# Fused attention, mixture of experts and MLP: another order for the first and last attention slots, and weight loads held back behind the second expert's tokens

## The chip, the cores and the metric

The kernel runs on 1 core of one Trainium2 chip. The metric is device time of the whole program in microseconds (us). TensorE is PE, VectorE DVE, ScalarE ACT, GpSimd POOL and SyncE SP. SP computes nothing; it issues most of the DMAs, in the order of the program. Each engine works off its own queue strictly in order. Where a queue is meant that only issues DMAs, the profile writes SPq, ACTq or POOLq.

## The reference, cut to what matters

Three stages follow each other: a decayed linear attention in blocks, a mixture of 8 experts of which each token takes one, and an MLP.

```python
for b in range(nb):                                  # attention, 2 batches x 8 heads, 768 x 64
    intra = (qb @ kb.T * Dmask) @ vb
    inter = (qb * lam_pow) @ kv_state
    out[:, :, sl] = intra + inter
    kv_state = lam_block * kv_state + (kb * rev_pow).T @ vb
x = out as [1536 tokens, 512]
logits = (x / |x|) @ (emb / |emb|).T / tau           # routing: 8 experts, the largest wins
for e in range(8):
    out[mask_e] = gate_w * (relu(x[mask_e] @ w1[e]) @ w2[e])      # 512 -> 1024 -> 512
h = x @ w_in; g = elu(h); y = g @ w_out              # 512 -> 2048 -> 512
```

## The kernel before, in words

**Attention in slots.** The 1,536 tokens are 12 slots of 128 (6 chunks of 128 positions, 2 batches; slot s is chunk s // 2 of batch s % 2). A slot's q, k and v arrive as one 1 MB tile in two DMAs of 512 KB (`load_a`, `load_b`, L333 to L344). Per slot there are these steps, each a nested function of `attention`:

- `stage_a` (L346, PE): keys times queries into the PSUM tile `st`. `mask` (L357, DVE): two multiplications of `st` with the decay mask `Dm` into `stm`. `keys` and `queries` (L365, L374, POOL): decayed keys `kd` and queries `qd`.
- `stage_b` (L382, PE): state `St` times `qd` (L390) and values times `stm` (L397) into `xp`; ACT then copies it to `xs` (L402). The state has to be up to date for the slot two before.
- `products` (L409, PE L417, POOL L422) and `add` (L426, DVE L432): the slot's contribution to the state.
- `stage_c` (L434), a generator that is advanced one step at a time. Step 1: PE turns `xs` into token-major form and takes the expert logits with it, into `tm` (L439, "the turn" below). Step 2: DVE sums the logits `lg` (L443). Step 3: ACT squares, accumulates and takes the root (L448, L449). Steps 4 and 5: DVE `nrm` and `rs` (L451, L455). Step 6: ACT writes the normalised row's upper half (L459). Step 7: DVE the lower half (L462), and SP writes the row to the DRAM tensor `rows` (L465), twice for slots 0 to 3.

The order is written out by hand: the program order is the order of each engine's queue. In the loop over s (L507 to L538) slot s does `queries`, `stage_a`, `mask`, `keys`, then `stage_c(s - 2)`, `stage_b(s - 1)` and `products(s - 1)`. Slots 10 and 11 and the routing are a list written out after the loop (L540 to L575).

**Start.** `powers` (L273) makes the decay powers `zs` and writes them from ACT's queue to a DRAM tensor `Z`; `masks` (L288) reads `Z` back as a skewed view, from SP's queue, into `Dm`. SP has issued slots 0 and 1 before that and issues slots 2 to 5 behind it.

**Weights.** Every weight piece (1 MB of float32) is loaded into one of 5 raw buffers by `load` (L125) and split by `preparing` (L147) into two float16 halves, in two chunks a piece: an ACT operation (L157, 128x1024) for the upper half and, one step later, a DVE operation (L161) for the lower. A chunk that ends a piece calls `load` for the next one. In attention, `ATT_LOADS` and `ATT_STEPS` (L50, L51) name the slots in which a load or one step is put between the attention work; later `tick` (L206) hands out steps by a budget.

**Routing and the first expert.** `top` and `route` (L607, L631) find each token's expert and its place among that expert's tokens, by small DVE operations and small PE products, here for the slot groups 0 to 7, 8 to 10 (`top` in two parts) and 11. `first_gather` (L674) makes indices of expert 0's tokens in slots 0 to 7 and fetches them from `rows` by two indirect DMAs of POOL (`gather`, L765; 128 rows, then 96 rows of 2 KB). `dispatch` (L699) adds those of slots 8 to 11 by one-hot products on PE (L721) and gives expert 0's tokens `x`.

**Experts.** `layer1(e)` (L937) has 96 matrix products for each expert (L949), `layer2(e)` 96 (L990), in the order layer1(0), layer1(1), layer2(0), layer1(2), ... After the first 24 of layer1(0), `route_end` (L753) makes the indices of all the other experts and issues `gather(1)`; after 72, `transpose(1)` turns the gathered tokens of expert 1 on PE (L933) and ACT copies them (L934). Later experts' tokens are turned by a DMA.

`manual_schedule` keeps this order, and two engines that touch one PSUM tile are kept in program order by semaphores, two readers too, as the trace shows for the tile `tm`.

Of the kernel before, what the change touches and what calls it, by code (L numbers as in the profile page):

```python
# [21 lines left out]
P = 128  # L22
# [27 lines left out]
ATT_LOADS = (2, 4, 5, 6, 7)  # L50
ATT_STEPS = range(4, 8)  # L51
# [14 lines left out]
class K:  # L66
    def __init__(self, ctx, tc, A, out, dbg=None):
        self.ctx, self.tc, self.nc, self.A, self.out = ctx, tc, tc.nc, A, out
        self.dbg = dbg or {}
        self.raws = {}  # L70
        self.wts = {}
        self.next_load = 0
        self.rings = [], []
        self.hold = False
# [50 lines left out]
    def load(self):  # L125

        if self.next_load >= len(self.units):
# [19 lines left out]
    def preparing(self):  # L147
# [21 lines left out]
        for i, h in self.units:  # L169
            while h == 0 and (self.hold or not self.w_free()):  # L170
# [5 lines left out]
            while (i, h) not in self.raws:  # L176
                self.load()
# [128 lines left out]
    def attention(self, ctx):  # L306
# [26 lines left out]
        def load_a(s):  # L333
# [6 lines left out]
            nc.sync.dma_start(t[:, 0:2], A["qkv"][s, :, 0:2])  # L340
            T[s] = t

        def load_b(s):
            return nc.sync.dma_start(T[s][:, 2:4], A["qkv"][s, :, 2:4])  # L344
# [60 lines left out]
        def state(s):  # L405
            products(s)
            add(s)

# [25 lines left out]
        def stage_c(s):  # L434
            xs = XS.pop(s)

            tm = ps_s.tile([P, KD, 256], F32, name=f"tm{s}", tag="st")
            for k in range(KD):
                nc.tensor.matmul(tm[:, k, 0 : P + E], xs[:, k, :], ie[:, k, :], start=True, stop=True)  # L439
            yield  # L440
            x = tm[:, :, 0:P]
            g = slice(s, s + 1)
            nc.vector.tensor_reduce(  # L443
                out=lg[:, s, :], in_=tm[:, :, P : P + E].rearrange("p k e -> p e k"), axis=AX.X, op=ALU.add
            )
            yield
            sq = ap.tile([P, KD, P], F32, name=f"sq{s}", tag="sq", bufs=1)
            nc.scalar.activation(out=sq, in_=x, func=AF.Square, accum_out=ss[:, g])  # L448
            nc.scalar.activation(out=yr[:, g], in_=ss[:, g], func=AF.Sqrt)  # L449
            yield  # L450
# [3 lines left out]
            yield  # L454
            nc.vector.reciprocal(out=rs[:, g], in_=nrm[:, g])  # L455
            yield
            row = ap.tile([P, 2, DM], F16, name=f"row{s}", tag="row", bufs=NS - FIRST)
            hi, lo = (row[:, j].rearrange("p (k c) -> p k c", c=P) for j in range(2))
            nc.scalar.activation(out=hi, in_=x, func=AF.Copy, scale=rs[:, g])  # L459
            self.row[s] = row  # L460
            yield
            nc.vector.scalar_tensor_tensor(out=lo, in0=x, scalar=rs[:, g], in1=hi, op0=ALU.mult, op1=ALU.subtract)  # L462
# [13 lines left out]
        for s in range(2):  # L476
            load_a(s)
            load_b(s)
        warm(6)
        zt, zs = self.powers(a1, ps_r)  # L480
        self.masks(a1, zt)
        self.scales(a1, zs)
        load_a(2)
        load_b(2)
        nc.scalar.dma_start(self.c32[:, 128:], A["c32"][:, 128:])
        for s in range(3, 6):
            load_a(s)
            load_b(s)
# [17 lines left out]
        run = lambda g: [None for _ in g]  # L506
        for s in range(1, 10):  # L507
            if s > 1:
                if s in IN_AT:
                    load_a(IN_AT[s])  # L510
                    load_b(IN_AT[s])
                if s in ATT_LOADS:
                    self.load()
                queries(s)
                if s > 2:
                    stage_a(s)
                mask(s)
                keys(s)
            c = stage_c(s - 2) if s > 1 else iter(())
            if s == 2:  # L520
                next(c), next(c)
                stage_b(s - 1)
                run(c)
            else:
                if s > 3:


                    next(c), next(c), next(c)
                    add(s - 2)
                    next(c), next(c)  # L530
                    if s in ATT_STEPS:
                        self.step()
                run(c)
                stage_b(s - 1)
            state(s) if s == 1 else s > 2 and products(s - 1)
# [4 lines left out]
        c8, c9, c10, c11 = (stage_c(s) for s in range(8, NS))  # L540
        t7, t9, t10, t11 = (self.top(*g, a1) for g in ((0, 8), (8, 10), (10, 11), (11, 12)))
        r7, r10, r11 = (self.route(*g, a1, ps_r) for g in ((0, 8), (8, 11), (11, 12)))
# [3 lines left out]
        go(t7, t7, t7, t7)  # L546
        queries(10)
        stage_a(10)
        mask(10)
        go(r7, c8, c8)  # L550
        add(8)
        go(c8, r7, r7, r7, c8, c8)
        stage_b(9)
        products(9)
        go(fg, c8, fg, c8)
        queries(11)
        stage_a(11)
        mask(11)
        self.group += 1
        go(c9, c9)  # L560
        add(9)
        go(c9, fg, fg, c9, c9)
        stage_b(10)
        self.finished("in10")
        go(t9, t9, t9, t9, c9, c9)
        self.step()
        go(c10, c10, t10, c10, t10, c10, t10, c10, t10)
# [3 lines left out]
        go(r10, r10, put, c10, c10)  # L571
        self.step()

# [762 lines left out]
```

## Time and profile before

| | us |
|---|---|
| median of 3 runs (504.83 to 507.26) | 506.09 |
| the profiled execution's own time | 507.02 |
| its span | 505.1 |
| PE busy (share of the span) | 471.9 (93%) |
| DVE busy | 345.1 (68%) |
| ACT busy | 230.1 (46%) |
| POOL busy | 73.0 (14%) |

Times below are from the start of the span. In a line of the timeline the columns are the start, the duration, engine, line, operation, the tiles written and read, the count, and in brackets how long the engine had been idle and what ended that.

### The profile page before, as it was taken

To read this page: it belongs to the slowest core of one execution; us is meant where nothing else is said; L and a number is where in the kernel's file an instruction comes from. 1 tells how busy PE (TensorE), PEld (TensorE's weight loads), DVE (VectorE), ACT (ScalarE), POOL (GpSimd) and SP (SyncE) were. 2 spreads that over 40 slices of the span, in tenths; PEclk is the share of its full clock that TensorE was granted. 3 is DMA by queue.
4 is the path that set the end of the run, shared out by engine and by line. 5 is a ranking of instruction groups with operands and counts; after the bars stand their busy time and mean duration, and the time that the engine had idled before them with its cause. 6 is when DMAs were issued, how large, how long until landed. Compare 5 with 4: busy or idle time off the path is not lost. (4 is left out here: it accounts for less than half of the span.)

```text
span 505.1 us, 9103 instructions
## 1 busy us (share of the span) xinstructions
PE 471.9 (93%) x3678; PEld 332.3 (66%) x3678; DVE 345.1 (68%) x612; ACT 230.1 (46%) x382; POOL 73.0 (14%) x66
## 2 busy tenths in 40 slices
PE   6789976689999999999999999999999999999993
PEld 6688865589999999999644444444444444445561
DVE  3469775849999957999787897889544435345352
ACT  1156433768785665333364444535242333333341
POOL 4359520502103100000000000000000003003020
PEclk9799987979999999999999999999999999999997
DMA  6999923599999979956522220000000002002010
GB/s 220 377 404 405 404 96 126 202 283 307 303 381 295 345 289 307 328 182 215 190 84 83 84 84 1 0 1 1 0 1 0 1 0 84 0 2 84 1 62 27
DMA packets 27959, 79.09 MB, mean 157 GB/s; under 512 B 13280, under 2 KB 14848, under 8 KB 21768
## 3 DMA queue, kind: packets, MB, share of 16 engines
q1 hardware_dynamic: 25280, 70.63, 41.2%
q0 software_dynamic: 2288, 7.61, 4.2%
q8 instruction: 31, 0.51, 0.4%
q10 hardware_dynamic: 344, 0.21, 0.2%
q14 instruction: 16, 0.13, 0.1%
HBM read 68.33 MB, written 7.36 MB: 150 GB/s over the span
## 5 line engine op out<-in xcount | busy, mean ns | idle before, releaser
L1034 PE MATMUL pf<-yT,w 128*128 128x512 f16 (+2 forms) x672 | 133.4, 349 | 0.6 <-DVE yT L1000 0.6
L1074 PE MATMUL po<-w,g 128*128 128x512 f16 x576 | 133.3, 379 | 0.3 <-DVE g L1060 0.3
L1034 PEld LDWEIGHTS <-w 128*128 128x128 f16 x672 | 62.4, 98 | 66.0 <-issue 0.9
L1044 DVE TENSOR_TENSOR et<-pf,bc 128x512 f32<-128x512 f32 (+2 forms) x56 | 34.4, 615 | 97.0 <-PE pf L1034 94.8
L1074 PEld LDWEIGHTS <-g 128*128 128x128 f16 x576 | 55.9, 98 | 66.1 <-DVE g L1060 1.2
L1045 ACT ACTIVATE eu<-et 128x512 f32<-128x512 f32 (+2 forms) x56 | 31.9, 569 | 139.8 <-DVE et L1044 139.8
L161 DVE SCALAR_TENSOR_TENSOR w<-raw,w 128x1024 f16<-128x1024 f32 x64 | 76.6, 1228 | 17.8 <-ACT w L157 17.8
L949 PE MATMUL ph<-x,w 128*128 128x224 f16 x768 | 76.9, 262 | 0.5 <-DVE x L749 0.5
L949 PEld LDWEIGHTS <-w 128*128 128x128 f16 x768 | 74.6, 99 | 1.5 <-issue 0.7
L990 PE MATMUL py<-h,w 128*128 128x224 f16 x768 | 74.7, 259 | 0.0
L990 PEld LDWEIGHTS <-w 128*128 128x128 f16 x768 | 73.4, 98 | 0.2 <-issue 0.2
L157 ACT ACTIVATE w<-raw 128x1024 f16<-128x1024 f32 x64 | 64.4, 1051 | 2.2 <-DVE cs L882 2.1
L1093 POOL DMA_INDIRECT out<-o,idx x12 | 12.0, 1004 | 285.4 <-DVE o L1091 276.8
L769 POOL DMA_INDIRECT g<-rows,idx x16 | 22.8, 1428 | 91.0 <-DMA x<-g 60.0
L1060 DVE SCALAR_TENSOR_TENSOR g<-et,g 128x512 f16<-128x512 f32 (+2 forms) x56 | 34.0, 608 | 0.2 <-ACT g L1054 0.2
L1053 DVE SCALAR_TENSOR_TENSOR et<-eu,et 128x512 f32<-128x512 f32 (+2 forms) x56 | 33.9, 605 | 0.3 <-ACT eu L1046 0.3
L1046 ACT ACTIVATE eu<-eu 128x512 f32<-128x512 f32 (+2 forms) x56 | 31.9, 570 | 1.8
L1054 ACT ACTIVATE g<-et 128x512 f16<-128x512 f32 (+2 forms) x56 | 30.9, 552 | 0.2 <-DVE et L1053 0.2
L157 ACT ACTIVATE w<-cv 128x1024 f16<-128x1024 f32 x16 | 16.9, 1054 | 23.7 <-DVE cv L226 23.7
L957 ACT ACTIVATE h<-ph 128x448 f16<-128x448 f32 x32 | 16.7, 541 | 11.2 <-PE ph L949 11.2
L996 ACT ACTIVATE yT<-py 128x448 f32 (+1 forms) x16 | 8.7, 541 | 24.7 <-PE py L990 19.9
L226 DVE SCALAR_TENSOR_TENSOR cv<-raw,cv 128x1024 int32<-128x1024 int32 x16 | 19.5, 1220 | 0.2
(187 smaller groups left out, 405.8 us busy)
## 6 DMA issues: line engine op xcount, KB each, us to landing
raw<-w SPq DMA_DIRECT2D x32, 1024.0 KB, 6.8
in<-qkv SPq DMA_DIRECT2D x16, 512.0 KB, 6.7
raw<-wi SPq DMA_DIRECT2D x8, 1024.0 KB, 5.0
raw<-wo SPq DMA_DIRECT2D x8, 1024.0 KB, 5.1
win<-qkv SPq DMA_DIRECT2D x8, 512.0 KB, 10.6
rows<-row SPq DMA_DIRECT2D x16, 256.0 KB, 7.4
bc<-cd POOLq DMA_DIRECT2D x1, 768.0 KB, 7.7
Dm<-Z SPq DMA_DIRECT2D x1, 512.0 KB, 4.2
```

The source lines that it names most:

```text
L157: nc.scalar.activation(out=o[0], in_=x, func=AF.Copy, scale=sc)
L161: nc.vector.scalar_tensor_tensor(out=o[1], in0=x, scalar=sc, in1=o[0], op0=ALU.mult, op1=ALU.subtract)
L949: nc.tensor.matmul(ps[:, j, :], w[:, wl, k, c : c + P], x[:, xl * KD + k, :], start=(n == 0), stop=(n == 11))
L990: nc.tensor.matmul(ps[:, j, :], w[:, wl, f % 4, c : c + P], h[:, hl, f, :], start=(n == 0), stop=(n == 23))
L1034: nc.tensor.matmul(ps[:, :n], w[:, wl, k, c : c + P], yT[yl][:, k, t0 : t0 + n], start=(i == 0), stop=(i == 11))
L1044: nc.vector.tensor_tensor(out=t[:, :n], in0=UT[m, f][:, :n], in1=self.bc[:, t0 : t0 + n], op=ALU.mult)
L1045: nc.scalar.activation(out=u[:, :n], in_=t[:, :n], func=AF.Relu, scale=-1.0)
L1046: nc.scalar.activation(out=u[:, :n], in_=u[:, :n], func=AF.Exp, scale=-1.0)
L1053: nc.vector.scalar_tensor_tensor(out=t, in0=u, scalar=-1.0, in1=t, op0=ALU.add, op1=ALU.max)
L1054: nc.scalar.activation(out=g[:, 0, :n], in_=t, func=AF.Copy, scale=S_G)
L1060: nc.vector.scalar_tensor_tensor(out=g[:, 1, :n], in0=t, scalar=S_G, in1=g[:, 0, :n], op0=ALU.mult, op1=ALU.subtract)
L1074: nc.tensor.matmul(acc[t], g[:, gl, t * P : t * P + P], w[:, wl, f % 4, :], start=(f == first and i == 0), stop=(f == last and i == 2),)
```

## The change

At the start slot 0 alone is loaded from SP ahead of `Z`; slot 1's two DMAs move to ACT's queue behind `Z`, and the rest of the constants behind them. The first two slots' `products` and `add` come ahead of the first masks, with 8 dummy products (`warm`) between. The constants `c16` and `iota1` are loaded at slot 4. The first raw weight is loaded at slot 3 where it was slot 2, and there is a fifth step at slot 8. `stage_c` is cut into functions; within a slot the square now stands ahead of the logits' sum, and the weight step behind the upper half of the row, where it was ahead of it. The two steps in the last slots are gone. Slots 8 to 11 are routed in one group. Row 8 is written ahead of the first gather. `route` computes `d` last, and the second one-hot table reuses a constant tile, where it took a weight buffer (`hold`, L848). From the first expert on, `load` only counts what is owed; the loads are issued from ACT's queue behind `transpose(1)`.

```diff
-ATT_LOADS = (2, 4, 5, 6, 7)
-ATT_STEPS = range(4, 8)
+ATT_LOADS = (3, 4, 5, 6, 7)
+ATT_STEPS = range(4, 9)
...
-    def load(self):
+    def load(self, eng=None, now=False):
+        if now:
+            self.owed -= self.late
+        elif self.late:
+            self.owed += 1
+            return
...
-            nc.sync.dma_start(r, (self.A["w1"], self.A["w2"])[w // 2][e, w % 2])
+            (eng or nc.sync).dma_start(r, (self.A["w1"], self.A["w2"])[w // 2][e, w % 2])
...
-        for s in range(2):
-            load_a(s)
-            load_b(s)
+        load(0)
         warm(6)
         zt, zs = self.powers(a1, ps_r)
+        load(1, nc.scalar)
+        nc.scalar.dma_start(self.c32[:, 128:], A["c32"][:, 128:])
         self.masks(a1, zt)
         self.scales(a1, zs)
-        load_a(2)
-        load_b(2)
-        nc.scalar.dma_start(self.c32[:, 128:], A["c32"][:, 128:])
-        for s in range(3, 6):
-            load_a(s)
-            load_b(s)
+        for s in range(2, 6):
+            load(s)
...
-        stage_a(0)
-        stage_a(1)
+        for s in range(2):
+            stage_a(s)
+            products(s)
+            add(s)
+        warm(8)
         mask(0)
-        state(0)
-        stage_a(2)
         mask(1)
-        nc.sync.dma_start(self.c16, A["c16"])
-        nc.sync.dma_start(self.iota1, A["i1"])
...
+        stage_b(0)
+        for s in range(2, 10):
+            if s in IN_AT:
+                load(IN_AT[s])
+            if s == 4:
+                nc.sync.dma_start(self.c16, A["c16"])
+                nc.sync.dma_start(self.iota1, A["i1"])
+            if s in ATT_LOADS:
+                self.load()
+            queries(s)
+            stage_a(s)
+            mask(s)
+            keys(s)
+            turn(s - 2)
+            squares(s - 2)
+            logits(s - 2)
+            if s > 3:
+                add(s - 2)
+            norms(s - 2)
+            high(s - 2)
+            if s in ATT_STEPS:
+                self.step()
+            low(s - 2)
+            stage_b(s - 1)
+            if s > 2:
+                products(s - 1)
...
+        t8, t12 = (self.top(*g, a1) for g in ((0, FIRST), (FIRST, NS)))
+        r8, r12 = (self.route(*g, a1, ps_r) for g in ((0, FIRST), (FIRST, NS)))
...
+        queries(10)
+        stage_a(10)
+        turn(8)
+        squares(8)
+        go(t8, t8, t8, t8)
+        mask(10)
+        go(r8)
+        stage_b(9)
+        logits(8)
+        add(8)
+        queries(11)
+        stage_a(11)
+        products(9)
+        norms(8)
+        high(8)
+        go(r8, r8)
+        mask(11)
+        turn(9)
+        squares(9)
+        go(r8)
+        add(9)
+        stage_b(10)
+        self.finished("in10")
+        go(fg)
+        low(8)
+        go(fg)
+        logits(9)
+        norms(9)
+        high(9)
+        stage_b(11)
...
+        low(9)
+        go(fg, fg)
+        turn(10)
+        squares(10)
+        logits(10)
+        norms(10)
+        high(10)
+        turn(11)
+        logits(11)
+        squares(11)
+        go(t12, t12, t12, t12)
+        go(put, r12)
+        low(10)
+        go(r12)
+        norms(11)
+        high(11)
+        go(put, put)
+        low(11)
+        go(put)
+        go(r12, r12, r12, r8)
...
                 if e + 1 < E and fp == (0 if e else 2):
                     transpose(e + 1)
+                    if e == 0:
+                        self.late = False
+                        for _ in range(self.owed):
+                            self.load(nc.scalar)
                     if e + 2 < E:
                         self.gather(e + 2)
```

In the last list `go(put)` stands, in turn, for: nothing yet; the one-hots of slots 8 and 9; those of 10 and 11 and the products of the gathered tokens; the products of slots 8 to 11 and the copies to `x`.

## Rows read from the trace of the kernel before

**Rows 1.** The page's second part: what the DMA engines moved, in 40 slices.

```profile
GB/s 220 377 404 405 404 96 126 202 283 307 303 381 295 345 289 307 328 182 215 190 84 83 84 84 1 0 1 1 0 1 0 1 0 84 0 2 84 1 62 27
```

**Rows 2.** Stretches of 1 us: length, busy time (instructions) by engine, PE's granted clock, DMA share, GB/s.

```profile
10.00:11.00 1.00, 0.60 (x16) 0.46 (x16) 0.96 (x2) 0.00 (x0) 0.95 (x1) 1.00 0.18 47
...
16.00:17.00 1.00, 1.00 (x8) 1.00 (x10) 1.00 (x2) 0.00 (x0) 0.91 (x1) 0.50 1.05 430
...
21.00:22.00 1.00, 1.00 (x8) 1.00 (x8) 0.96 (x3) 0.00 (x0) 1.00 (x1) 0.79 1.02 418
```

**Rows 3.** Timeline: the write of the decay powers and the skewed read.

```profile
5.14 0.29 ACTq L285 DMA_DIRECT2D Z<-zs  x1
...
9.60 0.39 SPq L292 DMA_DIRECT2D Dm<-Z  x1
```

**Rows 4.** Timeline: the first raw weight's issue; DMA issues of that moment: us to landing.

```profile
22.00 0.33 SPq L135 DMA_DIRECT2D raw<-w  x1
...
raw<-w SPq DMA_DIRECT2D x1, 1024.0 KB, 9.5
```

**Rows 5.** Timeline, slots 5 to 7 and the start of slot 10.

```profile
35.12 1.19 PE L439 MATMUL tm<-ie,xs 128*128 128x136 f32 x8
...
39.72 1.19 PE L439 MATMUL tm<-ie,xs 128*128 128x136 f32 x8
...
41.37 0.18 DVE L443 TENSOR_REDUCE lg<-tm 128x8 f32<-128x32 f32 x1
...
42.63 1.06 ACT L157 ACTIVATE w<-raw 128x1024 f16<-128x1024 f32 x1
...
44.16 0.59 ACT L402 ACTIVATE xs<-xp 128x512 f32<-128x512 f32 x1
...
44.80 1.19 PE L439 MATMUL tm<-ie,xs 128*128 128x136 f32 x8 [0.42 <-ACT xs L402]
...
57.50 0.71 PE L354 MATMUL st<-win 64*128 64x128 f32 x8
```

**Rows 6.** Waits of the first 110 us: us in total, times, longest.

```profile
ACT sq L448 <- DVE lg L443: 22.9, 11, 3.6
```

**Rows 7.** Groups by line and shape, 57.5 to 88.3 us: busy us, mean ns, idle before.

```profile
L721 PE MATMUL px<-oh,row 128*128 128x224 f16 x32 | 5.1, 335 | 0.0
...
L462 DVE SCALAR_TENSOR_TENSOR row<-tm,rs,row 128x512 f16<-128x512 f32 x5 | 3.7, 749 | 2.1 <-ACT row L459 2.1
...
L362 DVE TENSOR_TENSOR stm<-st,Dm 128x512 f32<-128x512 f32 x4 | 2.6, 684 | 0.9 <-PE st L354 0.9
...
L448 ACT ACTIVATE sq<-tm 128x512 f32<-128x512 f32 x4 | 2.4, 598 | 10.2 <-DVE lg L443 10.2
...
L432 DVE TENSOR_TENSOR S<-S,kr 64x256 f32<-64x256 f32 x4 | 1.7, 413 | 0.0
...
L669 DVE TENSOR_TENSOR ohb<-c,bb 128x1024 f16<-128x1024 f32 x1 | 1.2, 1217 | 0.0
```

**Rows 8.** DMA issues (us to landing): the last row, the first gather; timeline: expert 0's start.

```profile
rows<-row SPq DMA_DIRECT2D x1, 256.0 KB, 2.3
...
g<-rows,idx POOLq DMA_INDIRECT x2, 3.6
...
88.27 2.47 PE L949 MATMUL ph<-x,w 128*128 128x224 f16 x24 [0.52 <-DVE x L749]
```

**Rows 9.** Timeline and waits, 86 to 135 us: expert 1's tokens and what follows.

```profile
92.70 13.85 SPq L135 DMA_DIRECT2D raw<-w  x4
...
93.86 1.87 POOL L769 DMA_INDIRECT g<-rows,idx  x1 [0.30 <-issue]
...
PE pt L933 <- DMA g<-rows,idx: 5.8, 2, 3.4
...
102.95 13.51 PE L949 MATMUL ph<-x,w 128*128 128x224 f16 x120
...
125.53 9.36 PE L949 MATMUL ph<-x,w 128*128 128x224 f16 x96
```

More of the change, by code (lines that the diff above doesn't have):

```diff
@@ L73, in __init__ @@
         self.rings = [], []
-        self.hold = False
+        self.late, self.owed = False, 0
         self.units = [(i, h) for i in ORDER for h in range(1 if i < 4 * E else 2)]
@@ L169, in preparing @@
         for i, h in self.units:
-            while h == 0 and (self.hold or not self.w_free()):
+            while h == 0 and not self.w_free():
                 t = chunk()
@@ L432, in add, with turn, logits, squares @@
                     nc.vector.tensor_tensor(out=St[b][r, :, r], in0=St[b][r, :, r], in1=kv[r], op=ALU.add)
[L434 removed]
+        TM = {}
+        def turn(s):
             xs = XS.pop(s)
[L437 removed]
+            tm = TM[s] = ps_s.tile([P, KD, 256], F32, name=f"tm{s}", tag="st")
             for k in range(KD):
                 nc.tensor.matmul(tm[:, k, 0 : P + E], xs[:, k, :], ie[:, k, :], start=True, stop=True)
[L440 to L441 removed]
+        def logits(s):
+            nc.vector.tensor_reduce(
+                out=lg[:, s, :], in_=TM[s][:, :, P : P + E].rearrange("p k e -> p e k"), axis=AX.X, op=ALU.add
+            )
+        def squares(s):
             g = slice(s, s + 1)
[L443 to L446, printed above, removed]
             sq = ap.tile([P, KD, P], F32, name=f"sq{s}", tag="sq", bufs=1)
[L448 removed]
+            nc.scalar.activation(out=sq, in_=TM[s][:, :, 0:P], func=AF.Square, accum_out=ss[:, g])
             nc.scalar.activation(out=yr[:, g], in_=ss[:, g], func=AF.Sqrt)
[L450 removed]
+        def norms(s):
+            g = slice(s, s + 1)
             nc.vector.tensor_scalar(
@@ L497, in attention @@
         keys(1)
-        stage_a(0)
-        stage_a(1)
+        for s in range(2):
[3 more added lines that the diff above has]
+        warm(8)
         mask(0)
-        state(0)
-        stage_a(2)
         mask(1)
-        nc.sync.dma_start(self.c16, A["c16"])
-        nc.sync.dma_start(self.iota1, A["i1"])
[L506 to L535, printed above, removed]
+        stage_b(0)
[24 more added lines that the diff above has]
+                products(s - 1)
             if s - 1 in IN_W:
@@ L672, in route @@
         )
+        yield
+        nc.vector.tensor_tensor(out=rt["d"][:, g], in0=l, in1=bc8(mx), op=ALU.subtract)
     def first_gather(self, a1, ps_r):
@@ L724, in products, with gathered @@
                 )
-        places(FIRST, NS - 1)
-        yield
-        places(NS - 1, NS)
-        yield
-        pts = [ps_s.tile([P, 2, 2, 256], F32, name=f"px{i}", tag="st") for i in range(2)]
+        pts = [ps_s.tile([P, 2, 2, 256], F32, name="px0", tag="st"), None]
         g0, g1 = self.G.pop((0, 0)), self.G.pop((0, 1))
         at = lambda k: pts[k // 4][:, k // 2 % 2, k % 2]
-        for i in range(2):
-            ks = range(KD * i, KD * i + KD)
+        def gathered(ks):
             for k in ks:
@@ L742, in dispatch @@
                 )
-            for s in range(FIRST, NS - 1):
-                products(s, ks)
-            yield
+        yield
+        pts[1] = ps_s.tile([P, 2, 2, 256], F32, name="px1", tag="st")
+        places(FIRST, FIRST + 2)
+        yield
+        places(FIRST + 2, NS)
+        for i in range(2):
+            gathered(range(KD * i, KD * i + KD))
+        yield
+        for s in range(FIRST, NS - 1):
+            products(s)
         for b in range(2):
@@ L847, in route_sorted @@
             )
-        self.hold = True
-        while not self.w_free():
-            yield
-        self.hold = False
-        ohb = self.w_tile("ohb").bitcast(BF16).rearrange("p a k f -> p (a k f)")
-        ohb = ohb[:, 0 : NS * P].rearrange("p (s c) -> p s c", c=P)
+        ohb = rt["ohb"].bitcast(BF16)
         nc.vector.tensor_tensor(
@@ L1005, in moe_mlp @@
         self.budget = 0.0
+        self.late = True
         self.sorting = self.route_sorted(rp, rhs, ps_a)
```

50 lines of the change are left out of this document (14 added, 36 removed).

## The prediction

> **What bounds the kernel now.** I read the page's slices first, then short stretches, the timeline and the list of waits. The slices [rows 1] show two stages with different limits. From about 16 to 63 us the DMA engines move 404 to 430 GB/s, the most of the whole run [rows 1, 2]: slots and raw weights fill SP's queue, and whatever is put into it lands only when all that stands before it has landed. From 103 us PE works without a gap: one layer of one expert is 96 products in 9.36 us, and the next starts at once [rows 9]. So time is won in two places only: ahead of 88.27 us, where expert 0's products start [rows 8], and in the hole around expert 1's tokens, where PE waits 5.8 us in two pieces [rows 9]. Everything later moves along with these. I split the sum into three terms: A, up to the start of slot 10's `stage_a` at 57.50 [rows 5]; B, from there to 88.27, that is 30.8 us; C, the hole.
>
> **Term A, start.** `Z` is issued at 5.14 and `Dm`, which waits for it, only at 9.60 [rows 3]: this write of 8 KB lands 4.4 us later, just as the 2 MB of slots 0 and 1 run out. Then the DMA engines stand almost still, 47 GB/s [rows 2], for about two microseconds. With slot 1 behind `Z`, only the rest of slot 0 is ahead of it; I take the shortest landing of a write here, 2.3 us [rows 8], so `Dm` is issued near 7.4. Its landing still has slot 1's 1 MB beside it. The two states are added while `Dm` is on its way (they took DVE 4 x 0.41 us [rows 7], now ahead of the masks). The 8 dummy products run while PE would wait for the first mask; without that cover they cost up to 2.4 us (8 at a turn's rate, 1.19 for 4 [rows 5]). I estimate that slot 4 begins 1 to 5 us earlier than before, likeliest 4 to 5. How much it is matters little, because of what follows.
>
> By the Trainium skill ("DMA: Bandwidth & Descriptors", Queues, rings and completion order) a DMA engine serves the queues that have work in turns, packet by packet. By that rule `Z` on ACT's queue would not have waited for slots on SP's, and moving slot 1 would bring `Dm` nothing; the gain of the sum would be 0.9 us smaller, -3.0. The 4.4 us of `Z` speak against it.
>
> **Term A, the first weight.** Before, the first raw weight is issued at 22.00 and lands 9.5 us later, at 31.5 [rows 4]. Now row 0's two writes (2 x 0.26 MB) and slot 7 (1.05 MB) stand ahead of it, and `c16` with `iota1` (0.21 MB) no longer: 1.36 MB more, at 0.41 MB/us 3.3 us. The stream itself starts sooner: I put the hole at 1.2 us where it was 2, so 0.9 us back. It lands at 33.9. The first weight step needs it in slot 4, and behind that step in ACT's queue stands the copy `xs` of slot 3, which the next turn on PE needs. The step takes about 1.0 us (1.06 in [rows 5]), from `xs` to the turn it is 0.64 (44.16 to 44.80) [rows 5]. So slot 3's turn starts at 33.9 + 1.0 + 0.6 = 35.5; before it was 35.12 [rows 5]. The lead of the start is used up in waiting for a DMA: +0.4. Bounds: if the weight landed without delay, the lead of up to 5 us would stay; if no hole were saved, 1 us more.
>
> PE idles there for about as long as the lead was. After such a rest its clock is down: at 16 us, after a rest since 10.6, the granted clock is 0.50 (1.2 GHz of 2.4), and it is back only within the stretch 21 to 22 [rows 2]. Five microseconds at half speed do 2.5 us less work; I take +2.3 for this slot (bounds 0 and 2.7).
>
> **Term A, the slots with steps.** Before, a slot without delay takes 4.60 us from turn to turn (35.12 to 39.72), one in which ACT comes late 5.08 [rows 5]. In each of them the square waits for the logits' sum [rows 6], and the weight step fills ACT's gap while DVE makes the norm: 42.63, then upper half and `xs` 44.16 [rows 5]. Now the square comes first and the sum waits for it, and the step stands behind the upper half. Chain from turn to turn: turn 1.2 [rows 5], square 0.6 [rows 7], sum 0.2 [rows 5], state addition 2 x 0.41 [rows 7], norm and reciprocal 2 x 0.18 (taken as the sum's), 0.2 to ACT, upper half and step 1.5 (42.63 to 44.16, in the other order), `xs` to turn 0.64 [rows 5]: 5.5 us. Three such slots follow (turns 4 to 7): 16.5 us. Before they took 57.50 - 39.72 - 3.5 = 14.3, where 3.5 is a slot less `stage_a`. +2.2; bounds 0 (PE's 4.6 stays the longer) and 3. Term A is 0.4 + 2.3 + 2.2 = +4.9: slot 10 starts at 62.4.
>
> **Term B, the last slots.** I walk DVE's queue from the start of `stage_a(10)`. Slot 0 to 7's `top`, mask 10, the state of 8 and `norms` are done by 5 us, but the rank product's reading waits for PE's `products(9)`, in the same tile, at 6.5 (stage_b(9), stage_a(11), products: 3.7 us behind the mark at 2.4). Then two reductions 0.4, six small operations 1.2, mask 11 1.4, one-hot 1.2, state 9 0.8, low half of row 8 0.75 [rows 7]: 12.2. New here: row 8 is now written ahead of the first gather, so the gather waits for its landing, 2.3 us [rows 8] and 0.2 of issue: 14.7; on POOL nothing is queued behind it until expert 1's, on SP rows 9 to 11 are. The second of its DMAs starts 1.5 later and lands in 3.6 [rows 8]: 19.8; PE's 16 products on it end at 21.5. Beside that DVE does rows 9 and 10, the sums of 11, one `top` and one rank for four slots, and the one-hots: 8.5 us, and the low half of row 11 ends at 21.4. The two chains meet. The 32 products took 5.1 us [rows 7], mostly at the lower clock; I take 4.5 (bounds 3.1, at 96 in 9.36 [rows 9], and 5.1), and 0.7 for the copies. Expert 0 starts 26.7 us after slot 10, against 30.8: -4.1 (bounds -2.5 and -5.5). What is gone is mainly two weight steps on DVE, two rounds of `top` and `route`, and the stop of PE ahead of `stage_a(11)`.
>
> **Term C, expert 1's tokens.** Today four raw loads are issued from 92.70 on, the second gather DMA at 93.86, 5.6 us after expert 0's start [rows 8, 9]. The turned tokens' products start at 102.95, so it lands near 102.2: 8.4 us, where the first gather, alone, took 3.6 [rows 8]. Without the raw loads I take 3.6, plus 0.9 for the longer issue (1.87 us [rows 9]), plus 0.5 for expert 2's gather, which POOL issues right behind: 5.0. It lands at 10.6, the products go on at 11.4, where they did at 14.7: 3.3 us. The 120 products there took 13.51 us; at 96 in 9.36 they are 11.7 [rows 9]. Of these 1.8 us I count 1.4. Term C: -4.7 (bounds -0.5 and -6.5). The two loads that are owed are issued behind ACT's copies, 0.33 us each as on SP [rows 4]; behind them waits the next relu, which PE needs 9 us later. The weights stay ahead of PE: a piece takes 2.6 us of DMA and 4.7 us of PE (48 products), and five are loaded by then. For the same reason the moved `d`, the sixth step that moves into the expert phase and the constant tile that replaces a weight buffer cost nothing; if the weights were late, each would show as PE's wait at L949.
>
> **Sum.** 4.9 - 4.1 - 4.7 = -3.9 us, from the profiled execution's 507.02 to 503.1. That execution is 0.9 above the median of the runs, 506.09; against the median it is 502.2.
>
> **Rivals.** (1) The lead stays, wholly or in part. If the first weight holds nobody up and the slots stay near 4.6, term A is about -5 and the time 492.3; if only the slot order is free of cost and the clock stays up, A is +0.4 and the time 497.7. For it: the order frees the square from DVE's queue. Against: the full DMA queue [rows 1]. 0.08 and 0.14. (2) Expert 1's tokens stay late: the gather's 0.19 MB have turns beside the raw loads already, at half of 0.41 MB/us 0.5 us are lost by them, and the rest is POOL's issue and expert 2's gather. C is -0.5, the time 506.4. For it: the issue took 1.87 us before any raw byte moved; against: 8.4 us is far more than 3.6 + 0.9. 0.13. The rule of turns cited above is what this rival goes by. (3) Slower: PE's clock stays at 1.2 GHz through the slots with steps, since PE now rests 0.9 us in each. A slot's work of 4.6 then takes some 8 us (five at half speed did 2.5 [rows 2]); three slots, 2.5 each beyond the chain of 5.5: +7.5, the time 509.7. It decides at slot 3's turn: without a long wait of PE there the clock has no reason to fall. Against it: 0.42 us of waiting at 44.80 did not lengthen the next turn [rows 5]. 0.10.
>
> **How the numbers follow.** The forecast has 0.48, of which 0.44 are faster by over 0.5% (2.5 us, about what a measurement of this kernel can tell) and 0.04 within. Rival 1 adds 0.22 to faster, rival 2 0.13 to the same, rival 3 0.10 to slower; mixtures of the bounds leave 0.04 for the same and 0.03 for slower. Faster 0.66, same 0.21, slower 0.13. The forecast's own range is 498.5 to 505.5; to hold 0.8 it reaches to 495 (most of rival 1's part with the raw wait) and to 507 (rival 2).
>
> **What would show it.** Right: the first weight operation (L157) waits for a DMA until 33 to 35 us; turns 4 to 7 come 5.3 to 5.6 us apart; `stage_a(10)` starts at 61 to 64; the first gather's issue waits for a DMA; expert 0 starts 25.5 to 28 us after slot 10; PE's wait at L933 is under 2.5 us. Wrong: slot 10 ahead of 57.5 (rival 1), over 4 us of waiting at L933 (rival 2), a granted clock of 0.5 from 36 to 60 us (rival 3), or PE waiting for weights at L949 behind 105 us.

## The result, and the profile after

The changed kernel takes 500.42 us (median of 4 runs, 497.92 to 500.95), the kernel before 505.46 beside it (504.48 to 507.26): a ratio of 0.9887, 95% interval 0.9842 to 0.9932. It is faster by 1.1%, with the interval clear of 1. The forecast was 502.2, with a range from 495 to 507. The profiled execution took 500.95, its span is 499.0, where 507.02 and 505.1 stood before. PE is busy for 474.2 us of it (95%), DVE for 342.3, ACT for 231.1, POOL for 77.5.

The time was split into three terms, and each can be read off three lines of PE's timeline. Term A, the start of slot 10's `stage_a`: 64.41 us, 57.50 before, so 6.9 lost. Term B, from there to expert 0's first product: 25.06, 30.77 before, so 5.7 won. Term C, from there to the first product of `layer2(0)`: 21.23, 28.06 before (116.33 - 88.27), so 6.8 won. Together 5.6 are won; the span is shorter by 6.1. The 0.5 left lies behind that point: 388.8 us before, 388.3 now. The experiments spread from 388.2 to 389.3 there, the kernel before with the hold alone among them (388.3), so it is not read as a gain.

The first fence is the timeline of the changed kernel around the first raw weight: SP's issue, ACT's first weight operation, the turns of slots 2 to 5 and the start of slot 10 (columns as ahead of the prediction).

```profile
26.46 1.14 SPq L140 DMA_DIRECT2D raw<-w  x1
...
35.20 1.06 ACT L162 ACTIVATE w<-raw 128x1024 f16<-128x1024 f32 x1 [2.84 <-DMA raw<-w]
...
28.36 1.19 PE L440 MATMUL tm<-ie,xs 128*128 128x136 f32 x8
...
36.80 2.18 PE L440 MATMUL tm<-ie,xs 128*128 128x136 f32 x8 [3.61 <-ACT xs L405]
44.26 1.19 PE L440 MATMUL tm<-ie,xs 128*128 128x136 f32 x8
49.75 1.19 PE L440 MATMUL tm<-ie,xs 128*128 128x136 f32 x8 [0.67 <-ACT xs L405]
...
64.41 1.16 PE L357 MATMUL st<-win 64*128 64x128 f32 x16
```

Slot 2's turn at 28.36 is 2.2 us ahead of before:

```profile
30.53 1.19 PE L439 MATMUL tm<-ie,xs 128*128 128x136 f32 x8 [1.55 <-ACT xs L402]
```

Slot 3's, at 36.80, is 1.7 behind [rows 5]: ACT waits 2.84 us for the weight, and PE, which needs the `xs` copy behind it in ACT's queue, 3.61. Then the turn itself takes 2.18 instead of 1.19. The stretches of 2 us say why (columns as in [rows 2]; the granted clock is the third number from the end):

```profile
34.00:36.00 2.00, 0.00 (x0) 0.00 (x0) 0.52 (x1) 0.80 (x1) 0.00 (x0) 1.00 1.04 411
36.00:38.00 2.00, 1.20 (x5) 1.20 (x6) 0.00 (x0) 0.75 (x2) 0.00 (x0) 0.51 1.06 419
38.00:40.00 2.00, 2.00 (x11) 2.00 (x10) 0.26 (x2) 0.89 (x3) 0.00 (x0) 0.50 1.03 418
40.00:42.00 2.00, 2.00 (x18) 1.78 (x18) 1.92 (x5) 0.89 (x2) 1.18 (x2) 0.50 1.02 396
42.00:44.00 2.00, 2.00 (x36) 1.93 (x34) 1.71 (x2) 1.24 (x2) 2.00 (x1) 0.79 1.05 423
```

PE rests for the whole of 34 to 36, and behind the rest the clock is 1.2 GHz of 2.4 for some 7 us. From 44.26 on the turns are 5.49 us apart, where they were 4.60 to 5.08 [rows 5], and the list of waits names the other order: before, ACT's square waited for DVE's sum [rows 6], now DVE's sum waits for the square, up to 5.2 us.

```profile
DVE lg L443 <- ACT sq L450: 13.4, 9, 5.2
...
PE pt L955 <- DMA g<-rows,idx: 1.4, 1, 1.4
```

The last line answers to the 5.8 us of [rows 9]. The timeline of the changed kernel there, from the first gather to `layer2(0)`, on POOL, PE and ACT's queue:

```profile
80.04 1.19 POOL L797 DMA_INDIRECT g<-rows,idx  x1 [9.54 <-issue]
...
94.79 1.91 POOL L797 DMA_INDIRECT g<-rows,idx  x1 [0.30 <-issue]
...
85.72 3.23 PE L745 MATMUL px<-oh,row 128*128 128x224 f16 x32
89.47 2.47 PE L971 MATMUL ph<-x,w 128*128 128x224 f16 x24 [0.52 <-DVE x L777]
...
98.82 0.51 PE L955 MATMUL pt<-c,g 96*128 96x96 f16 x8 [1.36 <-DMA g<-rows,idx]
99.17 11.67 PE L971 MATMUL ph<-x,w 128*128 128x224 f16 x120
110.70 9.36 PE L1017 MATMUL py<-h,w 128*128 128x224 f16 x96
...
99.38 0.82 ACTq L140 DMA_DIRECT2D raw<-w  x2
```

In the kernel before, the turn of the second gather's tokens and the start of `layer2(0)` stood here:

```profile
102.33 0.82 PE L933 MATMUL pt<-c,g 96*128 96x96 f16 x8 [3.39 <-DMA g<-rows,idx]
...
116.33 9.36 PE L990 MATMUL py<-h,w 128*128 128x224 f16 x96
```

The second gather now lands 4.0 us behind its issue at 94.79, where it took 8.5 (93.86 [rows 9] to 102.33). The owed raw weights start only at 99.38, and the 120 products take 11.67 us, the rate of 96 in 9.36, where they took 13.51 [rows 9].

### The profile page after: what moved, and what is told of

Same layout as the page of the kernel before. It is cut to its first block, busy times and chain, and to the rows that moved or that the text cites. A ratio compares the mean times of both kernels' runs of the same rounds, so it can differ in the third digit from the quotient of the medians.

```text
span 499.0 us, 9094 instructions
## 1 busy us (share of the span) xinstructions
PE 474.2 (95%) x3683; PEld 334.2 (67%) x3683; DVE 342.3 (69%) x595; ACT 231.1 (46%) x382; POOL 77.5 (16%) x66
## 5 line engine op out<-in xcount | busy, mean ns | idle before, releaser
L166 DVE SCALAR_TENSOR_TENSOR w<-raw,w 128x1024 f16<-128x1024 f32 x64 | 77.0, 1228 | 10.6 <-ACT w L162 10.5
L971 PE MATMUL ph<-x,w 128*128 128x224 f16 x768 | 75.1, 259 | 0.5 <-DVE x L777 0.5
L797 POOL DMA_INDIRECT g<-rows,idx x16 | 26.3, 1643 | 79.5 <-DMA x<-g 56.6
L1081 DVE SCALAR_TENSOR_TENSOR et<-eu,et 128x512 f32<-128x512 f32 (+2 forms) x56 | 33.9, 605 | 0.3 <-ACT eu L1074 0.3
L440 PE MATMUL tm<-ie,xs 128*128 128x136 f32 x96 | 15.6, 312 | 6.1 <-ACT xs L405 6.1
L999 DVE SCALAR_TENSOR_TENSOR h<-ph,h 128x448 f16<-128x448 f32 x32 | 19.7, 617 | 0.0
```

What stands on the lines that cost most here:

```text
L166: nc.vector.scalar_tensor_tensor(out=o[1], in0=x, scalar=sc, in1=o[0], op0=ALU.mult, op1=ALU.subtract)
L971: nc.tensor.matmul(ps[:, j, :], w[:, wl, k, c : c + P], x[:, xl * KD + k, :], start=(n == 0), stop=(n == 11))
L1081: nc.vector.scalar_tensor_tensor(out=t, in0=u, scalar=-1.0, in1=t, op0=ALU.add, op1=ALU.max)
```

## The experiments

All readings in one table. A is the start of slot 10, B the way from there to expert 0, C from there to `layer2(0)`, in us, from the profile of each run. Each ratio is to the kernel before as it was measured beside that run (medians of 505.46 to 506.31).

| kernel | median (runs) | ratio to before, 95% | A | B | C |
|---|---|---|---|---|---|
| before | 505.46 (4) | | 57.50 | 30.77 | 28.06 |
| changed | 500.42 (4) | 0.9887 (0.9842 to 0.9932) | 64.41 | 25.06 | 21.23 |
| changed, once more (e12) | 501.40 (6) | 0.9901 (0.9877 to 0.9925) | 64.22 | 26.90 | 21.29 |
| before + hold (e7) | 499.37 (4) | 0.9873 (0.9849 to 0.9896) | 57.26 | 31.44 | 21.59 |
| changed without hold (e3) | 504.99 (12) | 0.9993 (0.9975 to 1.0011) | 63.29 | 26.97 | 24.74 |
| weight at slot 2 (e1) | 498.43 (5) | 0.9865 (0.9839 to 0.9891) | 59.46 | 26.79 | 21.30 |
| old slot order (e2) | 499.95 (6) | 0.9887 (0.9859 to 0.9914) | 61.78 | 27.05 | 21.20 |
| e1 and e2 together (e5) | 494.56 (6) | 0.9787 (0.9756 to 0.9818) | 56.45 | 26.66 | 21.40 |
| PE busy while waiting (e6) | 501.06 (6) | 0.9904 (0.9878 to 0.9930) | 62.27 | 25.20 | 21.27 |
| row 8 behind the gather (e4) | 499.54 (6) | 0.9883 (0.9857 to 0.9909) | 63.93 | 23.34 | 21.31 |
| e1, e2 and e4 together (e9) | 491.95 (5) | 0.9730 (0.9708 to 0.9753) | 56.19 | 23.14 | 21.26 |
| e1 + slot 1 ahead of Z (e8) | 496.67 (5) | 0.9833 (0.9812 to 0.9855) | 59.06 | 24.98 | 21.25 |
| e9 + slot 1 ahead of Z (e10) | 492.20 (5) | 0.9728 (0.9704 to 0.9752) | 56.80 | 24.74 | 21.29 |
| e9 without dummies (e11) | 492.62 (5) | 0.9734 (0.9711 to 0.9758) | 56.96 | 24.62 | 21.28 |

**Is the hold the whole of term C?** The kernel before, with the hold alone:

```diff
+        elif self.late:
+            self.owed += 1
+            return
...
+                    if e == 0:
+                        self.late = False
+                        for _ in range(self.owed):
+                            self.load(nc.scalar)
```

> The kernel before with only the hold of the raw weights from the first expert on (counted, and issued from ACT's queue behind the second expert's tokens). It prices the third term alone. Theory: there the raw weights are issued 4.4 us behind expert 0's start, ahead of the second gather DMA, where the changed kernel without the hold issues them at 5.3, beside it; so the hold brings here the whole of the third term, from 28.06 us between expert 0's start and layer2(0) to 21.3 +- 0.7; time 505.9 - 6.7 = 499.2 +- 1.3. Rival (only the 3.5 us that the run without the hold gave back are the hold's, the other 3.3 come from the shorter order of the last slots): 24.5 us, time 502.4 +- 1.3.

499.37 us: 6.4 less than the kernel before beside it, 505.73. C falls from 28.06 to 21.59; A is 0.2 shorter and B 0.7 longer. The timeline of that kernel (lines moved by a few):

```profile
88.70 2.47 PE L955 MATMUL ph<-x,w 128*128 128x224 f16 x24 [0.53 <-DVE x L755]
...
98.41 0.51 PE L939 MATMUL pt<-c,g 96*128 96x96 f16 x8 [1.40 <-DMA g<-rows,idx]
98.76 11.66 PE L955 MATMUL ph<-x,w 128*128 128x224 f16 x120
...
110.29 9.36 PE L1001 MATMUL py<-h,w 128*128 128x224 f16 x96
...
94.30 1.87 POOL L775 DMA_INDIRECT g<-rows,idx  x1 [0.30 <-issue]
...
98.96 1.31 ACTq L141 DMA_DIRECT2D raw<-w  x3
```

So this part by itself is worth all that the whole change brings, and the rest of the change comes out at nothing or a small loss: 499.37 with it left out, 500.42 and 501.40 with it. The reverse, the changed kernel without the hold:

```diff
-        self.late = True
         self.sorting = self.route_sorted(rp, rhs, ps_a)
```

> The changed kernel without the hold: raw weights are issued from SP at once, as before, and nothing is owed. Theory: the gather of expert 1 shares the DMA engines with them again, lands 13 to 15 us behind expert 0's start instead of 9.4, PE waits 4.5 to 6 us for it and loses the clock; layer2(0) starts 26.7 to 28 us behind expert 0's start instead of 21.2; time 506 +- 1.2. Rival 2 of the prediction (the raw loads cost the gather 0.5 us, the win in the hole came from the shorter order of the last slots): layer2(0) starts 21 to 22.5 us behind, time 501 +- 1.

504.99 us, and its interval against the kernel before holds 1. C is 24.74, halfway:

```profile
95.58 1.91 POOL L797 DMA_INDIRECT g<-rows,idx  x1 [0.30 <-issue]
...
95.59 14.30 SPq L140 DMA_DIRECT2D raw<-w  x4
...
101.64 0.82 PE L955 MATMUL pt<-c,g 96*128 96x96 f16 x8 [3.22 <-DMA g<-rows,idx]
```

Here the raw loads are issued together with the second gather, which lands 6.1 us behind its issue; before they were issued 1.2 us ahead of it [rows 9], and it took 8.5 (93.86 to 102.33); held back, 4.0. The theory (4.5 us of waiting at the gather or more, C at 26.7 or more) was too high here (3.4 us of waiting), and rival 2 (a cost of 0.5 us) too low. In these three kernels the gather takes the longer, the further the raw loads are ahead of it.

**Where are the 6.9 us of term A lost?** Two edits, alone and together.

```diff
-ATT_LOADS = (3, 4, 5, 6, 7)
+ATT_LOADS = (2, 4, 5, 6, 7)
```

> The changed kernel with the first raw weight loaded at slot 2 again, as before; everything else as changed. Theory: in the changed kernel the weight, issued at 26.46 us behind slot 7 and row 0, lands at 35.2 and holds ACT for 2.84 us and with it the turn of slot 3 at 36.80; the clock of 1.2 GHz from 36 to 42 us follows from that rest. Issued at slot 2 it lands by 30 us, ACT waits for nothing, slot 3's turn comes at 33.9 +- 0.7, the stretch behind it runs at 2.4 GHz and slot 10 starts 4 to 5 us earlier, near 60; time 496.0 +- 1.2 against 500.4. The slots with steps stay at 5.5 us. Rival (the load only moves the queue: slot 7 now lands late instead, or the slots themselves are what ACT and PE wait for): slot 10 stays at 63 to 65 and the time within 1.3 us of 500.4.

```diff
             turn(s - 2)
-            squares(s - 2)
             logits(s - 2)
+            squares(s - 2)
...
-            high(s - 2)
             if s in ATT_STEPS:
                 self.step()
+            high(s - 2)
             low(s - 2)
```

> The changed kernel with the old order inside a slot (the logits' sum ahead of the square, the weight step ahead of the upper half). Theory: turn to turn in slots 4 to 7 is then 4.6 to 5.1 us instead of 5.5, three slots and the one behind them, so slot 10 starts 1.5 to 2.5 us earlier, near 62.3, while the wait for the raw weight stays (2 to 3 us at 35 us) and the clock's fall with it; time 498.4 +- 1.2. Rival (the length of a slot is set by something the order does not touch, PE's own products or the DMA queue): turns stay 5.4 to 5.5 us apart, time 500.4 +- 1.

The third kernel has both diffs.

> The changed kernel with the first raw weight loaded at slot 2 and the old order inside a slot, both. Theory (the two losses of the changed kernel ahead of slot 10 are separate and add up): no wait for the weight, turns 4.6 to 5.1 us apart from 33.9 on, so slot 10 starts at 57 +- 1 (59.46 with the weight alone, 61.78 with the order alone); from there to expert 0's start 26.9 as in those two, from there to layer2(0) 21.3; time 495.6 +- 1.3. Rival (the DMA queue, at over 400 GB/s until 62 us, is the next bound: the tiles of the last slots or the weights of the steps arrive no earlier): slot 10 at 59 to 60 with waits for a DMA, time 498 +- 1.

With the weight at slot 2 it is issued at 19.85, ACT waits for nothing, the clock stays at 1.00, and slot 10 starts at 59.46: 4.8 to 5.0 us earlier, as expected. With the old order alone the turns are 4.59, 4.85 and 4.60 us apart (2.4 less in three slots) and slot 10 starts at 61.78; the wait for the weight stays. Together slot 10 starts at 56.45, 8.0 us earlier than in the changed kernel. Two turns of the kernel with the weight alone, in PE's timeline:

```profile
33.83 1.19 PE L440 MATMUL tm<-ie,xs 128*128 128x136 f32 x8 [0.67 <-ACT xs L405]
39.32 1.19 PE L440 MATMUL tm<-ie,xs 128*128 128x136 f32 x8 [0.67 <-ACT xs L405]
```

And those of the kernel with both, 4.59 apart where ACT is in time, once 5.55 where it is not:

```profile
33.36 1.19 PE L440 MATMUL tm<-ie,xs 128*128 128x136 f32 x8
37.95 1.19 PE L440 MATMUL tm<-ie,xs 128*128 128x136 f32 x8
43.50 1.19 PE L440 MATMUL tm<-ie,xs 128*128 128x136 f32 x8 [0.88 <-ACT xs L405]
```

The medians follow together (494.56, expected 495.6) but not one by one: e1 gives 2.0 against the first measurement of the changed kernel and 3.0 against the second, where 4.4 were expected, e2 0.5 and 1.5, where 2 were. By the profiles of e2 and of the changed kernel 2.0 us went back in B, 27.05 against 25.06. The next run says why. It is the changed kernel, once more.

> The changed kernel itself, once more, beside the others on one chip. Theory (the two halves of the last slots take 25.0 or 26.9 us, by where in them PE's clock falls, and the first profile showed the shorter one): slot 10 starts at 63 to 64.5, expert 0 25 to 27 us behind it, layer2(0) 21.2 behind that; time 500.4 +- 1. Rival (the first result was off): a median outside 499.2 to 501.6.

501.40 us, with B at 26.90. PE rests in two places in the last slots. The first rest, ahead of the last state products, is 1.90 us in both executions. The second is made up of pieces ahead of the gathered tokens, up to 1.7 us each. In the first execution the clock falls behind the first rest, in the second one only behind the second place. The turns of slots 10 and 11 in the first execution, and the stretch around them:

```profile
79.30 2.65 PE L440 MATMUL tm<-ie,xs 128*128 128x136 f32 x16
...
78.00:80.00 2.00, 2.00 (x17) 1.67 (x14) 0.89 (x4) 0.58 (x1) 0.00 (x0) 0.50 0.03 10
```

The same turns in this one, with the one-hot products and expert 0's start:

```profile
78.06 2.12 PE L440 MATMUL tm<-ie,xs 128*128 128x136 f32 x16
...
86.04 4.56 PE L745 MATMUL px<-oh,row 128*128 128x224 f16 x32
91.12 2.48 PE L971 MATMUL ph<-x,w 128*128 128x224 f16 x24 [0.52 <-DVE x L777]
```

4.56 us for the 32 products instead of 3.23, and 1.8 for B in all. Of the six other kernels with the same last slots, e6 and e8 show the short form and e1, e2, e3 and e5 the long one; the changed kernel shows each once. Why the clock falls behind the first rest in some executions and not in others no row here shows. Against the second execution, of the same form, e1's `layer2(0)` starts 4.9 us earlier (107.55 against 112.41), which is the expected price of the weight.

Is it the rest that lowers the clock at 36 us? The changed kernel with dummy products in that rest:

```diff
             keys(s)
+            if s == 5:
+                warm(16)
             turn(s - 2)
```

> The changed kernel with 16 dummy products (128x128, float32) ahead of slot 3's turn, where PE waits 3 to 4 us for the raw weight; nothing else is moved. It prices the clock's fall there alone. Theory: the weight is as late as before (ACT waits 2.6 to 3.1 us for it), but PE has not rested, so the granted clock from 36 to 42 us stays at 1.00 and the next turn comes 5.5 us later instead of 6.5 to 7.5: slot 10 starts 0.8 to 2 us earlier than in the changed kernel (62.2 to 63.4); time 499.2 +- 1.2. Rival (the fall has another cause than the rest, or the slot's 7.46 us come from the late weight itself): clock 0.5 again, time 500.4 +- 1.

PE's timeline, with the dummies, slot 3's turn and the next:

```profile
33.09 3.84 PE L479 MATMUL kr<-ones 128*128 128x128 f32 x32
36.76 1.09 PE L440 MATMUL tm<-ie,xs 128*128 128x136 f32 x8
...
42.15 1.19 PE L440 MATMUL tm<-ie,xs 128*128 128x136 f32 x8 [0.67 <-ACT xs L405]
```

The turn is as late (36.76) and the clock 1.00 from 34 to 44 us: 5.39 us to the next turn, where the changed kernel has 7.46 in one execution and 6.48 in the other. The wait for the weight is as long as before (2.72 us), so the rest of PE is the cause, and the fall costs 1.1 to 2.1 us; slot 10 starts at 62.27, some 2 us earlier. The median, 501.06 against 501.40 beside it, can't tell this from nothing: the runs lie in two heaps, three from 499.3 to 500.1 and three from 502.0 to 502.4, as the two forms of B would put them.

**What sets expert 0's start?** Row 8 written behind the first gather:

```diff
         go(fg)
-        low(8)
         go(fg)
+        low(8)
```

> The changed kernel with row 8 written behind the first gather instead of ahead of it. Theory: the gather's issue waits for the landing of the last row written ahead of it, so it is issued 2 to 3 us earlier, at 77 to 78 us instead of 80.0, and the products on it start earlier; but DVE's chain of rows 9 to 11 and the one-hots of the last slots ends no earlier, so expert 0 starts at most 1.5 us earlier: time 499.6, from 498.7 to 500.8. Rival A (the gather alone sets expert 0's start): expert 0 starts 2.5 us earlier, time 497.9. Rival B (rows were landing in time anyway): gather stays at 80, time 500.4.

The gather is issued at 76.32 (77 to 78 were expected), 12.4 us behind slot 10 instead of 15.6. PE no longer rests for it, the 32 products take 3.23 us, and B is 23.34. What PE then waits for, 0.70 us, is DVE's one-hots. In this execution the clock stays up behind both rests. Held against the second execution of the changed kernel, whose clock is up behind the first rest too, B is 3.6 us shorter: there the gather, with the clock behind it, set expert 0's start, and the theory's 1.5 and rival A's 2.5 were both too low. Where the clock falls behind the first rest the edit is worth little: e10 and e11 below have it too and show that form, with B at 24.74 and 24.62, where the kernels without it have 24.98 to 25.20. The median, 499.54, is 0.9 under the first measurement of the changed kernel and 1.9 under the second. The same edit on top of the two of term A:

> The changed kernel with the first raw weight at slot 2, the old order inside a slot, and row 8 written behind the first gather. Theory: slot 10 starts at 57 +- 1; the first gather is issued 2 to 3 us earlier than with row 8 ahead of it, PE does not rest ahead of the products on the gathered tokens, so the 32 one-hot products run at 2.4 GHz (3.2 us against 4.4 to 4.7) and expert 0 starts 23.4 +- 0.7 us behind slot 10, as in the run with row 8 alone; then 21.3 to layer2(0); time 492.2 +- 1.5, faster than both kernels. Rival (the profile of row 8 alone fell lucky: its median is only 0.9 under the changed kernel's): expert 0 starts 25.5 to 27 us behind slot 10, time 494.5 to 496.

491.95 us, 2.7% under the kernel before (interval 2.5 to 2.9%) and faster than the changed kernel. All three terms are as expected; here too the clock stays up behind both rests of the last slots. Its timeline, with the gather, slot 10, the one-hot products and the starts of expert 0 and `layer2(0)`:

```profile
68.37 1.19 POOL L797 DMA_INDIRECT g<-rows,idx  x1 [6.29 <-DVE idx L710]
...
56.19 1.16 PE L357 MATMUL st<-win 64*128 64x128 f32 x16
...
75.58 3.23 PE L745 MATMUL px<-oh,row 128*128 128x224 f16 x32 [0.70 <-DVE oh L737]
79.33 2.47 PE L971 MATMUL ph<-x,w 128*128 128x224 f16 x24 [0.52 <-DVE x L777]
...
100.59 9.36 PE L1017 MATMUL py<-h,w 128*128 128x224 f16 x96
```

**What does the new start bring?** Slot 1 ahead of `Z` again, in e1 and then in e9:

```diff
         load(0)
+        load(1)
         warm(6)
         zt, zs = self.powers(a1, ps_r)
-        load(1, nc.scalar)
```

> The run with the first raw weight at slot 2, with slot 1 loaded from SP ahead of the decay powers again, as in the kernel before. It prices the start alone. Theory: the write of the decay powers lands only when the 2 MB of SP's queue run out, so the skewed read is issued at 9.4 to 9.8 us instead of 6.8, the DMA engines stand still at 10 to 11 us, the turn of slot 2 comes 1.5 to 2.3 us later than 28.34, and slot 10 starts at 61 to 62 instead of 59.46; time 500.2 +- 1.3. Rival (the queues share the DMA engines in turns, so that two small writes pass beside the slots, and the earlier read came from something else): skewed read at 6.8 to 7.4, time 498.4 +- 1.

The timeline of the first, with the skewed read and slot 2's turn:

```profile
9.52 0.39 SPq L297 DMA_DIRECT2D Dm<-Z  x1
...
27.93 1.19 PE L440 MATMUL tm<-ie,xs 128*128 128x136 f32 x8
```

The theory was right on the queue and wrong on its price. The skewed read is issued at 9.52 again, 6.85 in e1. Yet slot 2's turn comes 0.4 us earlier, not later: the first mask begins at 15.4 us, behind the states on DVE, and the read is there by then. From the issue of `Z` to that of the read behind it pass 4.1 us (from 5.43) with 2 MB of slots issued ahead on the other queue, and 1.4 (from 5.48) in e1 with 1 MB. By the rule of turns that the Trainium skill states ("DMA: Bandwidth & Descriptors", Queues, rings and completion order), `Z` should have passed beside the slots in both; here the measurement decides against that. The median, 496.67 against 498.43, is 1.8 us lower; in the profiles most of the gain lies in B, 24.98 here, the short form.

> The fastest run so far (first raw weight at slot 2, old order inside a slot, row 8 behind the first gather) with slot 1 loaded from SP ahead of the decay powers again. Theory (from the run that undid the start alone: the skewed read was issued at 9.52 us instead of 6.85, yet the masks, which wait for the states, began at 15.4 instead of 15.8): the read is off the path once the states come ahead of the masks, so moving slot 1 behind it only delays that slot; the turn of slot 2 is 0.3 to 0.5 us earlier than 28.48 and the time 491.5 +- 1.2, not slower than 491.95. Rival (that run fell lucky, the late read costs): masks wait for the skewed read, slot 10 0.5 to 2 us later, time 492.5 to 494.

492.20 against 491.95: no difference that the intervals can tell. Slot 2's turn comes at 26.55, 1.9 us earlier than in e9, but 1.6 of it is the clock's. In e9's trace PE's clock is at 0.50 from 15 to 18 us in spite of the dummy products, which take 3.11 us there and 2.05 in e10:

```profile
14.09 3.11 PE L479 MATMUL kr<-ones 128*128 128x128 f32 x16 [1.02 <-DVE S L431]
```

The raw weight of e10, issued at 19.45, lands at 31.05, ACT waits 2.04 us for it and slot 3's turn is at 33.23 (33.08 in e9). The lead is lost to the DMA queue once more. The last run leaves the 8 dummy products ahead of the first masks out of e9:

```diff
-        warm(8)
         mask(0)
```

> The fastest run so far without the 8 dummy products ahead of the first masks. Theory: they do not delay stage_b of slot 0 by more than 0.7 us (it begins 0.7 us behind the first mask) and they fill PE's rest between 14.9 and 17.1 us; without them the rest is 2.2 us, the granted clock falls to 0.5 behind it in the stretch from 16 to 21 us as in the kernel before, and slot 10 starts 1 to 2.3 us later than 56.19; time 493.6 +- 1.3. Rival (a rest of 2.2 us leaves the clock up, as the rest of 1.9 us did in some of the runs ahead of the last turns): stage_b of slot 0 begins 0.7 us earlier and the time is 491.2 +- 1.2.

Stretches of 2 us, columns as above:

```profile
16.00:18.00 2.00, 1.10 (x9) 0.89 (x11) 2.00 (x4) 0.00 (x0) 1.81 (x3) 0.77 1.05 424
18.00:20.00 2.00, 2.00 (x16) 1.67 (x16) 0.44 (x1) 0.60 (x1) 1.08 (x1) 0.50 1.01 406
```

The clock falls to 0.50 as expected. Slot 2's turn is 1.1 us later than in e9 (29.59), slot 10 0.8 (56.96), where 1 to 2.3 were expected. But e9's clock had fallen there too. Against e5, whose start is the same and whose clock stays up, the turn is 0.8 later (28.76 there) and slot 10 0.5. The median, 492.62 against 491.95 (measured beside other runs), lies within the intervals, so only the profiles show this price. Of the other 2.5 us by which its span exceeds e9's, 1.5 lie in B, 24.62, where the clock falls behind the first rest as in e10, and not in e9; 1.0 lies behind the start of `layer2(0)`, at the top of the spread there.

## Why the prediction was right, step by step

The time and the sign of each term were right, and so were the mechanisms of the first weight, the slot order and the hold. The reason for the lead at the start was wrong, and most terms were sized too small. Three of the signs that the prediction named lie just outside their bounds: the wait for the weight to 35.2 (33 to 35), slot 10 at 64.4 (61 to 64), B at 25.1 (25.5 to 28).

- **Term A, forecast +4.9, measured +6.9 (6.7 in the second execution).** Step by step: slot 3's turn at 36.80, not 35.5 (+1.3); 7.46 us to the next at the low clock, not 6.9 (+0.6; 6.48 in the other execution); three slots of 5.49, 5.50 and 5.49, forecast 5.5; 3.67 to slot 10, not 3.5 (+0.2). The mis-sized step is the weight's landing: forecast 33.9, measured 35.2. It was reckoned at 0.41 MB/us throughout, but the engines moved 348, 279, 324, 221 and 344 GB/s in the five stretches from 27 to 32 us, 0.53 MB less than at that rate, which is the 1.3 us. This comes with the later load itself: from 27 to 32 us the six traces with the weight at slot 3 (the changed kernel twice, e2, e3, e4, e6) show 303 to 331 GB/s, the eight with it at slot 2 show 399 to 408. So the later load cost more than the bytes ahead of it. What in it slows the stream no row here shows. One stretch of the changed kernel and the same one of e1:

```profile
29.00:30.00 1.00, 1.00 (x11) 1.00 (x11) 0.77 (x2) 0.41 (x1) 0.21 (x1) 1.00 1.16 324
...
29.00:30.00 1.00, 1.00 (x11) 1.00 (x10) 0.75 (x2) 0.43 (x1) 0.20 (x1) 1.00 1.06 416
```

- **Term A, start.** Failed in its reason. The forecast let the earlier read of `Z` bring the lead and put it at 4 to 5 us. The lead was 2.2, and e8 shows that moving slot 1 brought none of it. The dummies are worth 0.8 of it (e11 against e5). The rest fits the states, which now stand ahead of the masks; no run undid that alone. As forecast, its size did not matter, since the weight took it back.
- **Term B, forecast -4.1, measured -5.7 and -3.9.** 26.7 us were forecast, with 4.5 for the 32 products; 26.90 and 4.56 were measured in the second execution, 25.06 and 3.23 in the first. So the mis-sized step of the first execution is mainly the 32 products, which were put mostly at the lower clock; the second, where they ran at it, is as forecast. The gather landed at 20.7 us behind slot 10, forecast 19.8. "The two chains meet" was off: in executions whose clock is up behind the first rest, B is 3.5 to 3.6 us shorter without row 8 ahead of the gather (e4 against e12, e9 against e5), so there the gather's chain was the longer.
- **Term C, forecast -4.7, measured -6.8 (-6.5 by the hold alone).** The gather lands 9.35 us behind expert 0's start, not 10.6 (4.0 behind its issue, where 5.0 were taken). 0.35 us pass from there to the products, not 0.8. And with a wait of 1.36 the clock does not fall, so all of 1.8 us comes back, not 1.4. Each remaining cost was put too high.
- **Rivals.** 1: slot 10 was not ahead of 57.5 and no lead stayed; with the weight early and the old order (e5) it is at 56.45. 2 is out: the hold alone brings 6.4 us. 3: the clock is back by 44 us, and rests of 0.67 in each slot do not lower it.

The sum, -5.6, is off by 1.7 from the forecast of -3.9, no more than a single term, because the errors have opposite signs: +2.0 in A against -1.6 in B and -2.1 in C. That they offset each other is luck.

## What to carry to other kernels

Look for bulk loads issued ahead of a gather that PE waits for: here the gather took 8.5 us behind them, 6.1 beside them and 4.0 without them. Holding them back until it has landed was the cheapest edit and worth more than all the others of the change. A lead at the start was worth only what the DMA queue let through: before work is moved earlier, look up when the transfer that it will need lands, and don't move that one later in the same edit. Where two edits of opposite sign share a change, time each alone: A lost what B won, and undoing the two losing parts and the early write of row 8 made 500.4 us into 492. And compare profiles only where the clock falls at the same place: two executions of one kernel differ by 1.8 us in B.

## What the runs showed of the hardware that was not expected

- The same two rests of PE in the last slots lowered its clock behind the first one in one execution and behind the second in another, 1.8 us apart in the end.
- At 5 to 10 us the granted clock is 1.00, yet the 6 dummy products of `warm(6)` (12 in the trace) took 2.93 us there in the changed kernel and most experiments, 2.01 in e7 and 1.60 in the kernel before, e2, e9 and e10. PE's early speed differs between executions by some 1.8 times, and the granted clock doesn't show it.
- The 8 dummies ahead of the first masks took 2.05 us in nine traces. In e2 and e9 they took 3.68 and 3.11: there the clock fell in spite of them.
- From the issue of `Z`, 8 KB on ACT's queue, to that of the read that waits for it passed 4.1 to 4.5 us with 2 MB issued ahead on SP's queue (four traces), and 1.4 to 2.0 with 1 MB (ten).
- With the first raw weight at slot 3 the DMA engines moved 303 to 331 GB/s from 27 to 32 us, with it at slot 2 399 to 408.
